# Performer attention and a feed-forward layer on one core: the beginning rebuilt (weight signs by Prelu, weight scales from squares, one shared key unit, other order)

## The chip, the cores and the metric

The kernel runs on one core of one Trainium2 chip. The metric is the device time of an execution in microseconds, as the median of several runs. The engines are named as in the profile: PE (matmul), PEld (its weight loads), DVE (vector), ACT (scalar, activations), POOL (GpSimd), SP (which issues the DMAs).

## The reference

```python
def _attn_ref(q, k, v, omega):                    # batch 8, heads 8, S = 576, D = 64, m = 128 features
    scale = 1.0 / np.sqrt(np.sqrt(D))
    def phi(x):
        h = np.einsum('bhsd,md->bhsm', x, omega) - np.sum(x * x, axis=-1, keepdims=True) / 2.0
        return np.exp(h - np.max(h, axis=-1, keepdims=True)) / np.sqrt(m)
    q_p, k_p = phi(q * scale), phi(k * scale)
    kv = np.einsum('bhsm,bhsd->bhmd', k_p, v)
    z = np.sum(k_p, axis=2)
    num = np.einsum('bhsm,bhmd->bhsd', q_p, kv)
    den = np.einsum('bhsm,bhm->bhs', q_p, z)[..., None] + 1e-06
    return num / den

def _moe_ref(x, w_in, w_out):                     # x: 4608 x 512, w_in: 512 x 2048, w_out: 2048 x 512
    h = x @ w_in
    return np.maximum(0.01 * h, h) @ w_out
```

The attention's output, heads side by side, is the x of the feed-forward layer. The weights come as 64-bit floats and are read as pairs of 32-bit words; the rest is 32-bit.

## The kernel before

The 4608 tokens are cut into 9 blocks of 512. For each block there is attention work (features of the queries, and the sums over keys and values of the batches that the block needs) and the feed-forward work: an "up" product with w_in (w1 in the program), the leaky maximum, a "down" product with w_out (w2). Blocks from 3 on use a seven-product scheme for the up product, and the last two for the down product too. Large products run as three 16-bit products of a high and a low part.

The beginning is what has to happen before the first up can start, and it has three strands.

- **Weights.** Each matrix comes in 8 pieces of 1 MB (`Weight.load`), 1024 64-bit numbers a partition. `Weight.convert` makes 32-bit floats of them from the upper and the lower word: ACT copies the upper word with a scale (L572), DVE shifts (L574) and puts three bits of the lower word in (L577), and the sign comes either from a Sign on ACT (L590) and a product on POOL (L592), or from another DVE pass (L595). PE sums the magnitudes against a column of ones (L585). `Weight.scale` needs all eight sums, takes the largest and makes a power of two of it with PE and DVE (`power_of_two`, L488 to L497). `Weight.split` then makes the high and low part of each piece.
- **Keys and values of batch 0.** A `Whole` unit takes one pair of heads: squares on ACT (L742), 32-bit projections on PE (L762), the maximum over features (L769) and a subtraction (L771) on DVE, the exponential on ACT (L773). Batches share a tile of 128 keys: batch 576 tokens is 4.5 tiles, so each unit of batch 0 has a fifth tile, projected apart into an "edge" buffer. The key sums (L865) multiply these with the values, which have been scaled by a power of two from their largest magnitude (L800, L457).
- **Queries of block 0.** The same unit, then PE turns the features (L953), the result is copied (L457), multiplied with the key sums (L982), divided (L992 to L995) into a block of x, cut into two 16-bit parts (ACT and POOL or DVE) and turned by a DMA (L910) into `xts`, of which an up needs all four.

The order of all this is not written by hand. Each operation is put on record with the engines that could do it, its buffers and a priority; `Plan.order` then lists the operations by a cost table, the priorities and long tables of corrections (`TURNS`, `HELD`, `ONLY`, by the number of the operation), with `LATER` and `PACE` for whole strands, and this is the order in which each engine's queue is written. Where the plan leaves PE a gap of 0.4 or more, `between` puts "fill" in the queue: matmuls on the identity that compute nothing and keep PE busy.

```python
                op("PE", 12 * 0.2165, up, r=[*(xts[j, k] for k in range(KT)),
                   *(key for k in range(KT) for key in w1.keys(4 * (f // 8) + k))], w=[ph], prio=work)
```

## Time and profile before

| | |
|---|---|
| runs, us | 928.76, 926.16, 928.54 (median 928.54) |
| span of the profiled execution, us | 926.5 (its own time is not listed apart; the median lies 2.0 above the span) |
| PE busy | 903.4 us |
| DVE busy | 770.4 us |
| ACT busy | 555.4 us |
| POOL busy | 387.1 us |
| granted clock of TensorE, mean | 0.997 |

A busy PE is not a working PE here: fill counts as busy, and so do matmuls at the lower clock. So the profile is read by stretches of time and by lines, not by the share of the span. Consecutive instructions of an engine overlap a little in the records; what one costs in a queue is the distance of the starts.

### The profile page before, as it was taken

The numbers are of one execution on the slowest core, as the hardware profiler recorded it, in microseconds if no ns is written. First come the engines' busy times: TensorE is split into PE (matmuls) and PEld (weight loads), VectorE is DVE, ScalarE is ACT, GpSimd is POOL, SyncE is SP. The second block draws the span as 40 slices with busy tenths as digits, with TensorE's granted clock in tenths as the row PEclk, the third lists the DMA queues.
The fourth block names the chain that finished last, engine by engine and source line by source line (L and its number), as shares of the span: only waits on it lengthen the run. The fifth ranks groups of instructions, "written<-read, shape, count | busy, mean of one in ns | idle before, by whom it ended". The sixth has DMA issues, their size and how long they took to land.

```text
span 926.5 us, 21317 instructions
## 1 busy us (share of the span) xinstructions
PE 903.4 (98%) x8660; PEld 620.5 (67%) x8660; DVE 770.4 (83%) x1374; ACT 555.4 (60%) x856; POOL 387.1 (42%) x342
## 2 busy tenths in 40 slices
PE   6989999999999999999999999999999999999998
PEld 5887465545555555578557855786568647888887
DVE  6989988997898977989887889889888886884772
ACT  4888586766673774658556745486457543542530
POOL 2234543556645453135502542134135456632650
PEclk9999999999999999999999999999999999999999
DMA  9684448756476589869686878489849645532401
GB/s 356 249 282 142 120 109 176 163 143 163 70 188 181 123 175 236 169 152 215 190 155 134 197 189 163 103 217 203 146 89 245 139 89 125 168 80 68 139 1 46
DMA packets 258242, 145.93 MB, mean 158 GB/s; under 512 B 191328, under 2 KB 238176, under 8 KB 257120
## 3 DMA queue, kind: packets, MB, share of 16 engines
q1 hardware_dynamic: 258144, 144.58, 63.4%
...
q14 instruction: 31, 0.25, 0.1%
...
## 4 chain that ended last, share of the span: by engine, by line
PE 81%; DVE 7%; DMA 6%; ACT 3%; issue 2%; POOL 1%; SPq 0%; DVEq 0%; ACTq 0%; POOLq 0%
PE fixps_ffn L1372 30%; PE fixps_ffn L1258 15%; PE fixps_ffn L1348 12%; PE lateps_ffn L1258 5%; PE attps_pj L698 5%; PE fixps_ffn L1182 4%; PE lateps_ffn L1182 4%; DMA proj_t<-proj_z 3%; DMA fix_big<-w_in 2%; PE attps_mi L975 1%; POOL fix_wt L592 1%; DVE fix_wt L577 1%; PE attps_mi L865 1%; PE attps_pj L762 1%; PE attps_mi L976 1%
## 5 line engine op out<-in xcount | busy, mean ns | idle before, releaser
L1372 PE MATMUL fixps_ffn<-fix_wt,fix_big 128*128 128x512 f16 x1344 | 302.6, 379 | 0.0
L1372 PEld LDWEIGHTS <-fix_big 128*128 128x128 f16 x1344 | 126.9, 98 | 144.1
L1258 PEld LDWEIGHTS <-fix_wt 128*128 128x128 f16 x2016 | 195.2, 98 | 27.1 <-issue 2.5
L463 POOL TENSOR_TENSOR fix_big<-fix_row,fix_big 128x512 f16<-128x512 f32 x100 | 133.8, 1344 | 179.2 <-ACT fix_big L457 165.2
L1258 PE MATMUL fixps_ffn<-fix_xt,fix_wt 128*128 128x256 f16 x1608 | 183.8, 273 | 2.1 <-DVE fix_row L1273 2.1
L1348 PE MATMUL fixps_ffn<-fix_xt,fix_wt 128*128 128x512 f16 x576 | 129.2, 379 | 0.8 <-ACT fix_row L1355 0.8
L1348 PEld LDWEIGHTS <-fix_wt 128*128 128x128 f16 x576 | 54.7, 98 | 63.8 <-issue 1.1
L717 ACT ACTIVATE att_p<-att_p,shift 128x1024 f32<-128x1024 f32 x68 | 69.9, 1030 | 36.8 <-DVE att_p L714 36.7
L705 DVE TENSOR_REDUCE proj_st<-attps_pj 128x8 f32<-128x1024 f32 x68 | 72.9, 1075 | 10.2 <-PE attps_pj L698 9.8
L457 ACT ACTIVATE fix_big<-fix_row 128x512 f16<-128x512 f32 x118 | 72.0, 623 | 9.7 <-DVE fix_row L1024 3.6
L714 DVE SCALAR_TENSOR_TENSOR att_p<-attps_pj,proj_sc,proj_st 128x1024 f32<-128x1024 f32 x68 | 76.6, 1132 | 0.1
L463 DVE TENSOR_TENSOR att_ph<-att_p,att_ph 128x1024 f16<-128x1024 f32 x56 | 73.9, 1323 | 2.2 <-ACT att_ph L457 2.2
L463 POOL TENSOR_TENSOR fix_xn<-fix_x,fix_xn 128x512 f16<-128x512 f32 (+1 forms) x24 | 26.1, 1089 | 94.7 <-ACT fix_xn L457 82.9
L1281 ACT ACTIVATE fix_row<-fix_row 128x512 f32<-128x512 f32 x69 | 43.1, 626 | 37.1 <-DVE fix_row L1273 36.7
L658 ACT ACTIVATE proj_z<-proj_nat 128x512 f32<-128x512 f32 (+1 forms) x56 | 36.2, 647 | 46.1 <-DMA proj_t<-proj_z 35.6
L1273 DVE TENSOR_TENSOR fix_row<-fix_row,fixps_ffn 128x512 f32<-128x512 f32 x57 | 38.9, 684 | 18.9 <-PE fixps_ffn L1258 9.7
L698 PE MATMUL attps_pj<-om,proj_t 64*128 64x128 f16 x1416 | 50.0, 217 | 4.0 <-DMA proj_t<-proj_z 3.2
L698 PEld LDWEIGHTS <-proj_t 64*128 64x128 f16 x1416 | 39.7, 94 | 18.9 <-issue 13.3
L682 DVE SCALAR_TENSOR_TENSOR proj_z<-proj_nat,proj_sc,proj_z 128x512 f16<-128x512 f32 (+1 forms) x52 | 50.8, 977 | 1.7 <-ACT proj_z L457 1.6
L457 ACT ACTIVATE att_ph<-att_p 128x1024 f16<-128x1024 f32 x47 | 49.2, 1047 | 0.9 <-PE attps_mi L878 0.5
L660 DVE TENSOR_REDUCE proj_sq<-proj_z 128x8 f32<-128x512 f32 (+1 forms) x56 | 39.4, 707 | 10.2 <-ACT proj_z L658 10.2
L1258 PE MATMUL lateps_ffn<-fix_xt,fix_wt 128*128 128x256 f16 x408 | 47.8, 273 | 0.0
...
## 6 DMA issues: line engine op xcount, KB each, us to landing
...
```

The source lines that it names most:

```text
L457: ("ACT", act(n, int(pointer)), lambda: nc.scalar.activation(dst(), src(), AF.Copy, scale=1.0 if scale is None else value()), False),
L463: return ways([(e, c, lambda g=g: g.tensor_tensor(dst(), a(), b(), op=ALU.subtract), True) for e, c, g in (("POOL", pool_(n), nc.gpsimd), ...
L682: op("DVE", stt(n) + 0.15, lambda: nc.vector.scalar_tensor_tensor(zl(), heads(), up(), zh(), op0=ALU.mult, op1=ALU.subtract), port=True, r ...
L698: nc.tensor.matmul(at(pj)[:, 512 * h + c * M:512 * h + (c + 1) * M], at(self.t)[r, 2 * (c0 + c) + x, :], om[r, w, :], start=(x + w == 0), ...
L705: op("DVE", dve(n * M), lambda: nc.vector.tensor_reduce(row(0), pv(), axis=AX.X, op=ALU.max), r=[pj], w=[st], prio=prio)
L714: op("DVE", dve(n * M), lambda: nc.vector.scalar_tensor_tensor(p(), pv(), down(), row(2).rearrange("p (g o) -> p g o", o=1).broadcast_to([ ...
L717: op("ACT", act(n * M, 1), lambda: nc.scalar.activation(flat(p()), flat(p()), AF.Exp, bias=shift), w=[p32], r=["ones"], prio=prio)
L1182: nc.tensor.matmul(o, ga(gp, f, 1)[:, 0, P * t:P * t + P], w(f, wp), start=(first and place + f % 2 + t + gp + wp == 0), stop=(place == 3 ...
L1258: nc.tensor.matmul(o, unit(at(wb[c]), u)[:, wp, P * a:P * a + P], mixes[j, c][n][1](xp), start=(first and a == 0 and i == 0), stop=(a == 1 ...
L1281: op("ACT", act(512), lambda: nc.scalar.activation(at(g), at(src), AF.Prelu, scale=H_DOWN_D if finish else H_DOWN_S, alpha=0.01), r=[src], ...
L1348: nc.tensor.matmul(at(ph), wk[wp][:, c:c + P], xt[:, xp, :], start=(i == 0), stop=(i == 3 * KT - 1))
L1372: nc.tensor.matmul(at(po), part(f, gp)[:, t * P:(t + 1) * P], wf[wp], start=(n == 0 and f % 4 == 0 and gp == wp), stop=(n == 3 and f % 4 = ...
```

## The change

- A weight piece is converted by a Prelu on ACT, whose slope of 2^32 for negative numbers sets the bit that the shift by three moves to the sign, a one-input pass on POOL that takes the top three bits of the lower word, and one DVE pass that joins both. The sign operations, the DVE shift and the choice `SIGN_POOL` go.
- The weight scale comes from squares: PE multiplies each 128-wide part of a piece with itself and adds all up in one bank; the largest sum's root gives the power of two.
- The fifth key tiles of batch 0 (for all four pairs of heads) are one unit "e" of their own, kept in two row buffers. The values of batches 0 and 1 stay unscaled; their scale comes from sums of squares on ACT and is applied where the key sums are evicted.
- The first queries are turned before their exponential, and the eviction is the exponential. Their products use the "ffn" banks, and every other x block a second buffer.
- For query block 1 and for edges, the scale, the bias and the exponential are one ACT instruction per head and tile (`powers`), without the DVE pass.
- The first three ups of block 0 are cut in two halves that need two `xts` each.
- All tables of the order are new.

```diff
-SIGN_POOL = {"w1": [0, 1, 3, 4, 5, 6, 7], "w2": [0, 1, 2]}
...
-PACE = {"k": 13.5, "q": 8.5, "w1": 0, "w1s": 0, "w2": 3.5, "w2s": 15.0}
+PACE = {'k': 20.5, 'q': 15.5, 'w1': 23, 'w1s': 0, 'w2': 8, 'w2s': 2}
...
-LATER = {"s": 0.0, "w1": -15.0, "w2": -275.0, "k": -5.0, "q": -565.0, "m": 0.0}
+LATER = {'s': 40.0, 'w1': -245.0, 'w2': -440.0, 'k': -700.0, 'q': -375.0, 'm': 1860.0}
...
+FUSED = (("q", 1),)
...
 TURNS = {
-    8: -220.529105, 10: -2270.804303, 11: -2600.332764, 14: -174.238138, 15: -156.646678, 17: -8199.116259,
...
+    4: -7005.2331, 7: -5110.3778, 15: -57900.145, 21: -5388.6643, 30: -5105.2668, 37: 5334.3764, 42: -2222.8973,
...
@@ class Weight: convert @@
-            op("ACT", act(1150), lambda: nc.scalar.activation(at(f), high().bitcast(F32), AF.Copy, scale=2.0 ** -112),
-               r=[b], w=[f], prio=prio)
-            op("DVE", dve2(1024), lambda: nc.vector.tensor_scalar(shifted(), bits(), 3, 0x7FFFFFF8,
-               op0=ALU.logical_shift_left, op1=ALU.bitwise_and), port=True, r=[f], w=[tmp], prio=prio)
-
-            op("DVE", stt(1024), lambda: nc.vector.scalar_tensor_tensor(shifted(), low(), 29, shifted(),
-               op0=ALU.logical_shift_right, op1=ALU.bitwise_or), port=True, r=[b], w=[tmp], prio=prio)
...
+            op("ACT", act(1150), lambda: nc.scalar.activation(at(f), high().bitcast(F32), AF.Prelu, scale=2.0 ** -112,
+               alpha=2.0 ** 32), r=[b], w=[f], prio=prio)
+            top3 = lambda: at(tmp).bitcast(U32)
+            ways([("POOL", pool_(1024), lambda: nc.gpsimd.tensor_scalar(top3(), low(), 2.0 ** -29, 7.0, op0=ALU.mult,
+                   op1=ALU.min), True)], r=[b], w=[tmp], prio=prio)
+            op("DVE", stt(1024), lambda: nc.vector.scalar_tensor_tensor(bits(), bits(), 3, top3(),
+               op0=ALU.logical_shift_left, op1=ALU.bitwise_or), port=True, r=[tmp], w=[f], prio=prio)
+
+            def squares():
+                half = at(f).bitcast(BF16).rearrange("p (a b) -> p a b", b=2)[:, :, 1]
                 for c in range(8):
-                    col = self.col0 + 4 * (8 * (i // 4) + c) + i % 4
-                    nc.tensor.matmul(at(self.sums)[:, col:col + 1], mag[:, c * P:(c + 1) * P], ones, start=True,
-                                     stop=True)
...
+                    x = half[:, c * P:(c + 1) * P]
+                    nc.tensor.matmul(at(self.sums)[:, :P], x, x, start=(i == 0 and c == 0), stop=(i == 7 and c == 7),
+                                     skip_group_check=True)
+            op("PE", 0.5, squares, r=[f], w=[self.sums], prio=prio, slack=6.0)
...
-            if i in SIGN_POOL[self.name]:
-                op("ACT", act(1130), lambda: nc.scalar.activation(at(f), high().bitcast(F32), AF.Sign), r=[b], w=[f],
-                   prio=prio)
-                op("POOL", pool_(1024), lambda: nc.gpsimd.tensor_tensor(at(f), at(tmp), at(f), op=ALU.mult), r=[tmp],
-                   w=[f], prio=prio)
-            else:
-                op("DVE", stt(1024), lambda: nc.vector.scalar_tensor_tensor(bits(), bits(), 0x80000000, shifted(),
-                   op0=ALU.bitwise_and, op1=ALU.bitwise_or), port=True, r=[tmp], w=[f], prio=prio)
...
@@ class Unit: features @@
+            if nt == 1 or fused:
+                def powers():
+                    for g in range(n):
+                        nc.scalar.activation(p()[:, g], pv()[:, g, :], AF.Exp, scale=down(), bias=row(2)[:, g:g + 1])
+                op("ACT", n * (act(M, 2) - 0.07), powers, r=[pj, st, self.sc], w=[p32], prio=prio)
+            else:
...
@@ class Whole: all_features @@
+            if self.what == "e":
+                self.ph = [buf("row"), buf("row")]
...
+                    op("DVE", dve(4 * M), lambda h=h, g=g: nc.vector.tensor_tensor(half(h), pv()[:, g], less(g).broadcast_to(
+                        [P, 4, M]), op=ALU.subtract), r=[pj, st], w=[self.ph[h]], prio=prio)
...
+            if self.what == "k":
+                op("ACT", act(n * M, 1), lambda: nc.scalar.activation(flat(p()), flat(p()), AF.Exp, bias=shift), w=[self.ph],
+                   r=["ones"], prio=prio)
...
@@ values @@
+            if b < WHOLE:
+                junk = buf("t")
+                op("ACT", act(half * D) + READ_SUM, lambda j=j, junk=junk: nc.scalar.activation(
+                   at(junk).rearrange("p a (b d) -> p (a b) d", d=D), at(raw)[:, j * half:(j + 1) * half, :D], AF.Square,
+                   accum_out=mx2[:, j:j + 1]), r=[(raw, j)], w=[junk, f"mx2_v{b}{j}"], prio=prio)
...
@@ query_block @@
-                    high(512, lambda qp32=qp32, i=i: qp32()[:, 512 * i:512 * i + 512], lambda turned=turned: at(turned),
-                         psum=True, r=[turned], w=[(qp, i)], prio=prio)
+                    op("ACT", act(512, 1), lambda qp32=qp32, i=i, turned=turned: nc.scalar.activation(
+                       qp32()[:, 512 * i:512 * i + 512], at(turned), AF.Exp, bias=shift), r=[turned, "ones"], w=[(qp, i)],
+                       prio=prio)
...
-                acc, r = buf("mi"), buf("r")
+                acc, r = buf("mi" if j else "ffn"), buf("r")
...
@@ feed_forward @@
+                steps = ((0, 1), (2, 3)) if j == 0 and f < 3 else (range(KT),)
+                for ks in steps:
+                    def up(f=f, ph=ph, ks=ks):
+                        for k in ks:
```

How the tables move instructions shows in the built programs. First DVE at the start of the weight and key work: in the names, attps_pj is a projection's bank, proj_st the maxima, att_ph, proj_edge and fix_row features, fix_wt weight pieces, fix_big raw ones. Before:

```order
L769 TENSOR_REDUCE proj_st_189<-attps_pj_173 128x8
L574 TENSOR_SCALAR fix_wt_65<-fix_wt_64 128x1024
L771 TENSOR_TENSOR att_ph_163<-attps_pj_173,proj_st_189 128x1024
L577 SCALAR_TENSOR_TENSOR fix_wt_65<-fix_big_88,fix_wt_65 128x1024
L769 TENSOR_REDUCE proj_st_190<-attps_pj_174 128x2
L771 TENSOR_TENSOR proj_edge_184<-attps_pj_174,proj_st_190 128x256
L574 TENSOR_SCALAR fix_wt_67<-fix_wt_66 128x1024
L574 TENSOR_SCALAR fix_wt_69<-fix_wt_68 128x1024
L577 SCALAR_TENSOR_TENSOR fix_wt_67<-fix_big_89,fix_wt_67 128x1024
L577 SCALAR_TENSOR_TENSOR fix_wt_69<-fix_big_90,fix_wt_69 128x1024
```

The same place of DVE's queue after the change:

```order
L766 TENSOR_REDUCE proj_st_187<-attps_pj_171 128x8
L787 TENSOR_TENSOR att_ph_161<-attps_pj_171,proj_st_187 128x1024
L766 TENSOR_REDUCE proj_st_188<-attps_pj_172 128x8
L775 TENSOR_TENSOR fix_row_94<-attps_pj_172,proj_st_188 128x512
L775 TENSOR_TENSOR fix_row_95<-attps_pj_172,proj_st_188 128x512
L766 TENSOR_REDUCE proj_st_189<-attps_pj_171 128x8
L787 TENSOR_TENSOR att_ph_162<-attps_pj_171,proj_st_189 128x1024
L575 SCALAR_TENSOR_TENSOR fix_wt_64<-fix_wt_64,fix_wt_65 128x1024
L575 SCALAR_TENSOR_TENSOR fix_wt_66<-fix_wt_66,fix_wt_67 128x1024
```

Two key units and the shared one now stand ahead of the first weight piece, which takes one pass instead of two or three.

Second, DVE around w1's scale (mx_w, pow_w). Before, five full units' reductions stand ahead of it:

```order
L769 TENSOR_REDUCE proj_st_189<-attps_pj_173 128x8
L995 TENSOR_TENSOR fix_x_84<-attps_mi_175,att_r_167 128x256
L605 TENSOR_REDUCE mxs_w_128<-fixps_ffn_113 128x16
L606 TENSOR_REDUCE mx_w_133<-mxs_w_128 128x1
L771 TENSOR_TENSOR att_ph_163<-attps_pj_173,proj_st_189 128x1024
L992 TENSOR_SCALAR att_r_168<-attps_mi_175 128x4
L993 RECIPROCAL att_r_168<-att_r_168 128x4
L492 TENSOR_REDUCE pow_w_134<-attps_mi_175 128x1
```

After, with eight reductions ahead of the scale:

```order
L766 TENSOR_REDUCE proj_st_187<-attps_pj_171 128x8
L766 TENSOR_REDUCE proj_st_188<-attps_pj_172 128x8
L590 TENSOR_REDUCE mx_w_131<-fixps_ffn_113 128x1
L787 TENSOR_TENSOR att_ph_162<-attps_pj_171,proj_st_187 128x1024
L787 TENSOR_TENSOR att_p_0_159<-attps_pj_172,proj_st_188 128x1024
L1016 TENSOR_SCALAR att_r_167<-fixps_ffn_114 128x4
L1017 RECIPROCAL att_r_167<-att_r_167 128x4
L488 TENSOR_REDUCE pow_w_132<-attps_mi_173 128x1
```

Two units (att_ph of the last keys of batch 0, att_p of the third queries) have moved ahead of the scale's last steps.

Third, PE at the first up (fix_xt are the turned x blocks, fix_wt the parts of w1; ident is fill). Before:

```order
L1423 MATMUL fixps_ffn_114<-ident 128x256
L1348 LDWEIGHTS fix_wt_80
L1348 MATMUL fixps_ffn_114<-fix_xt_99,fix_wt_80 128x512
...
L1348 MATMUL fixps_ffn_114<-fix_xt_100,fix_wt_65 128x512
...
L1348 MATMUL fixps_ffn_114<-fix_xt_101,fix_wt_67 128x512
...
L1348 MATMUL fixps_ffn_114<-fix_xt_102,fix_wt_71 128x512
...
L585 MATMUL fixps_ffn_113<-ones,fix_wt_70 128x1
```

After:

```order
L880 MATMUL attps_mi_173<-fix_v_109,att_ph_161 128x65 x4
...
L1374 MATMUL fixps_ffn_114<-fix_xt_99,fix_wt_80 128x512
...
L1374 MATMUL fixps_ffn_114<-fix_xt_100,fix_wt_65 128x512
...
L880 MATMUL attps_mi_173<-fix_v_109,att_ph_162 128x65 x4
...
L1374 MATMUL fixps_ffn_115<-fix_xt_99,fix_wt_80 128x512
...
L1447 MATMUL attps_pj_172<-ident 128x256
...
L1374 MATMUL fixps_ffn_114<-fix_xt_101,fix_wt_67 128x512
...
L1374 MATMUL fixps_ffn_114<-fix_xt_102,fix_wt_69 128x512
```

Two key sums of batch 1 and the first halves of two ups stand ahead of the first matmul that needs the third and fourth x block. Over the whole program the fill is 113 matmuls instead of 230, 107 of them up to this place. All other matmuls are as many as before, but that the 128 for the weight sums have 128 columns instead of one.

## Rows read from the trace of the kernel before

**Rows 1.** The page: the span, and the first line of part 1.

```profile
span 926.5 us, 21317 instructions
PE 903.4 (98%) x8660; PEld 620.5 (67%) x8660; DVE 770.4 (83%) x1374; ACT 555.4 (60%) x856; POOL 387.1 (42%) x342
```

**Rows 2.** Windows: four stretches; busy us per engine, granted clock, DMA share.

```profile
0.00:4.96 4.96, 0.00 (x0) 0.00 (x0) 1.40 (x7) 2.02 (x2) 0.20 (x4) 1.00 0.59 144
4.96:88.20 83.24, 76.92 (x844) 68.81 (x845) 74.57 (x117) 65.53 (x81) 26.38 (x18) 0.98 0.73 261
88.20:921.80 833.60, 826.40 (x7818) 551.69 (x7815) 693.17 (x1247) 487.81 (x774) 360.51 (x321) 1.00 0.63 148
921.80:926.50 4.70, 0.12 (x2) 0.00 (x0) 1.30 (x3) 0.00 (x0) 0.00 (x0) 0.81 0.16 56
```

**Rows 3.** Groups by line and form, PE, 5 to 88.2 us: fill.

```profile
L1423 PE MATMUL fixps_ffn<-ident 128*128 128x256 f16 x149 | 18.0, 274 | 0.0
L1423 PE MATMUL attps_pj<-ident 128*128 128x256 f16 x81 | 9.9, 276 | 0.0
```

**Rows 4.** DVE in time: start, us, what. Passes, w1's scale, last block.

```profile
37.23 1.22 DVE L769 TENSOR_REDUCE proj_st<-attps_pj 128x8 f32<-128x1024 f32 x1
38.36 0.68 DVE L574 TENSOR_SCALAR fix_wt<-fix_wt 128x1024 uint32<-128x1024 uint32 x1
38.96 1.22 DVE L771 TENSOR_TENSOR att_ph<-attps_pj,proj_st 128x1024 f32<-128x1024 f32 x1
...
47.26 0.15 DVE L497 TENSOR_SCALAR pow_w<-pow_w 128x1 f32<-128x1 f32 x1
...
82.13 0.42 DVE L995 TENSOR_TENSOR fix_x<-attps_mi,att_r 128x256 f32<-128x256 f32 x1
```

**Rows 5.** PE in time: key sums, the first up, weight sums.

```profile
36.17 1.11 PE L865 MATMUL attps_mi<-fix_v,att_ph 128*128 128x65 f32 x8
...
38.45 1.04 PE L953 MATMUL fixps_ffn<-ident,att_ph 128*128 128x128 f32 x8
...
88.21 2.75 PE L1348 MATMUL fixps_ffn<-fix_xt,fix_wt 128*128 128x512 f16 x12
90.80 0.34 PE L585 MATMUL fixps_ffn<-ones,fix_wt 128*128 128x1 bf16 x8
91.00 5.34 PE L1348 MATMUL fixps_ffn<-fix_xt,fix_wt 128*128 128x512 f16 x24
```

**Rows 6.** Windows: the early loads; DVE before and after w1's scale.

```profile
5.00:35.00 30.00, 27.28 (x300) 23.89 (x302) 25.00 (x39) 17.50 (x18) 8.53 (x8) 1.00 0.98 401
9.52:47.33 37.81, 34.93 (x422) 31.08 (x422) 34.51 (x50) 28.95 (x34) 13.26 (x11) 1.00 0.79 314
47.33:82.13 34.80, 31.48 (x333) 28.28 (x332) 31.83 (x47) 29.63 (x41) 10.83 (x6) 0.95 0.64 205
```

**Rows 7.** Groups by line and form, ACT, 5 to 88.2 us.

```profile
L572 ACT ACTIVATE fix_wt<-fix_big 128x1024 f32<-128x1024 f32 x13 | 14.9, 1147 | 7.1 <-DMA fix_big<-w_in 7.1
L590 ACT ACTIVATE fix_wt<-fix_big 128x1024 f32<-128x1024 f32 x10 | 11.3, 1158 | 0.6 <-DVE fix_wt L574 0.6
L773 ACT ACTIVATE att_ph<-att_ph,shift 128x1024 f32<-128x1024 f32 x9 | 10.3, 1146 | 1.4 <-DVE att_ph L771 1.4
```

**Rows 8.** Groups by line and form, POOL, 5 to 88.2 us.

```profile
L592 POOL TENSOR_TENSOR fix_wt<-fix_wt,fix_wt 128x1024 f32<-128x1024 f32 x9 | 22.3, 2486 | 36.8 <-DVE fix_wt L577 19.9 <-ACT proj_z L742 13.7 <-ACT fix_wt L590 1.9
```

**Rows 9.** Waits of PE from 88.2 us to the end.

```profile
PE attps_pj L698 <- DMA proj_t<-proj_z: 3.2, 3, 1.9
PE fixps_ffn L1258 <- DVE fix_row L1273: 2.1, 3, 0.9
```

**Rows 10.** Windows, PE alone: busy us, then granted clock.

```profile
64.00:66.00 2.00, 0.42 (x4) 1.00 0.57 178
68.00:72.00 4.00, 4.00 (x24) 0.58 0.00 0
```

More of the change, by code (lines that the diff above doesn't have):

```diff
@@ L166 @@
     HOP = {"PE": 0.25, "ACT": 0.08, "DVE": 0.08, "POOL": 0.10}
-    PRICE = {"PE": 1.0, "ACT": 1.28, "DVE": 8.28, "POOL": 1.0, "SP": 1.0}
+    PRICE = {'PE': 1.0, 'ACT': 2.464, 'DVE': 7.416, 'POOL': 4.818, 'SP': 1.0}
     def __init__(self, places, groups):
@@ L461, in low_ @@
     def low_(n, dst, a, b, engines=("DVE",), **of):
-        return ways([(e, c, lambda g=g: g.tensor_tensor(dst(), a(), b(), op=ALU.subtract), True)
-                     for e, c, g in (("POOL", pool_(n), nc.gpsimd), ("DVE", stt(n), nc.vector)) if e in engines], **of)
+        o = ways([(e, c, lambda g=g: g.tensor_tensor(dst(), a(), b(), op=ALU.subtract), True)
+                  for e, c, g in (("POOL", pool_(n), nc.gpsimd), ("DVE", stt(n), nc.vector))], **of)
+        if "POOL" not in engines:
+            o.price = {**o.price, "POOL": RARE}
+        return o
     def at(b):
@@ L770, in features @@
                prio=prio)
-            op("DVE", dve(n * M), lambda: nc.vector.tensor_tensor(p(), pv(), top().rearrange("p (g o) -> p g o",
-               o=1).broadcast_to([P, n, M]), op=ALU.subtract), r=[pj, st], w=[p32], prio=prio)
-            op("ACT", act(n * M, 1), lambda: nc.scalar.activation(flat(p()), flat(p()), AF.Exp, bias=shift), w=[p32],
-               r=["ones"], prio=prio)
-        def all_features(self):
-            self.ph = buf("ph")
-            self.p = lambda: at(self.ph).rearrange("p a b m -> p (a b m)").bitcast(F32).rearrange("p (g m) -> p g m",
-                                                                                                    m=M)
-            self.features(0, 4, self.ph, self.p)
-            if self.nt == VT:
-                self.edge = buf("edge")
-                self.features(4, 1, self.edge, lambda: edge32(self.edge))
+            less = lambda g: top()[:, g].rearrange("p (g o) -> p g o", o=1)
@@ new lines, in all_features @@
+            if self.what == "e":
+                self.ph = [buf("row"), buf("row")]
+                half = lambda h: at(self.ph[h]).rearrange("p (g m) -> p g m", m=M)
+                self.p = lambda g: half(g // 4)[:, g % 4]
+                for h in range(2):
+                    g = slice(4 * h, 4 * h + 4)
+                    op("DVE", dve(4 * M), lambda h=h, g=g: nc.vector.tensor_tensor(half(h), pv()[:, g], less(g).broadcast_to(
+                        [P, 4, M]), op=ALU.subtract), r=[pj, st], w=[self.ph[h]], prio=prio)
+                    op("ACT", act(4 * M, 1), lambda h=h: nc.scalar.activation(at(self.ph[h]), at(self.ph[h]), AF.Exp,
+                       bias=shift), w=[self.ph[h]], r=["ones"], prio=prio)
+                return
@@ new lines, in all_features @@
+            if self.what == "q":
+                self.ph = buf("p32")
+                p = lambda: at(self.ph)
+            else:
+                self.ph = buf("ph")
+                p = lambda: at(self.ph).rearrange("p a b m -> p (a b m)").bitcast(F32).rearrange("p (g m) -> p g m", m=M)
+            self.p = lambda g: p()[:, g]
+            op("DVE", dve(n * M), lambda: nc.vector.tensor_tensor(p(), pv(), less(slice(0, n)).broadcast_to([P, n, M]),
+               op=ALU.subtract), r=[pj, st], w=[self.ph], prio=prio)
@@ L812, in values @@
                w=[(both, "ones")], prio=prio)
-        for j in range(2):
+        for j in range(2 if b >= WHOLE else 0):
             s = slice(j * half, (j + 1) * half)
@@ L850, in key_batch @@
             u.all_features()
-            if u.nt == VT:
-                edges[b // 2, hp] = u.edge
-            edge = edges[b // 2, hp]
+            if not b and not hp:
+                edges[0] = Whole("e", b, hp, prio)
+                edges[0].all_features()
+            if b >= WHOLE:
+                if u.nt == VT:
+                    edges[b // 2, hp] = u.edge
+                edge = edges[b // 2, hp]
             if hp % 2 == 0:
@@ L1434, in performer_ffn @@
                     later(plan.opens[b.kind][b.place])
-            if o in fill:
+            if o in fill and fill[o][0].place < len(tiles[fill[o][0].kind]):
                 busy(*fill[o])
```

194 lines of the change are left out of this document (99 added, 95 removed), and 111 rows, old and new, of tables (HELD, TURNS).

## The prediction

> **What bounds the kernel now.** I read the page first: PE is busy for 903.4 of 926.5 us [rows 1]. But PE's time has two kinds of matmul in it, work and fill, so I cut the span into stretches next. Up to 4.96 us PE does nothing; from there to 88.20, where the first feed-forward matmul stands, it is busy for 76.92 of 83.24 us; from 88.20 to 921.80 for 826.40 of 833.60; the last 4.70 us are eviction and store [rows 2]. The groups by line say what the 76.92 us are: 149 and 81 matmuls on the identity, which compute nothing, take 18.0 + 9.9 = 27.9 us [rows 3]. So before 88.2 PE works for 76.9 - 27.9 = 49.0 us and loses 27.9 to fill and 6.3 to waiting; after 88.2 it loses 7.2 us in all. The reader is to see that PE's order decides everything after the beginning, and that the only large sum to be had is the 34.2 us (27.9 + 6.3) that PE doesn't work between 5 and 88 us.
>
> What holds the first feed-forward matmul (the first "up") back is the other engines' queue. DVE is busy for 74.57 of these 83.24 us, ACT for 65.53, POOL for 26.38 [rows 2]. In time: the weight scale of w1 is ready on DVE at 47.3 us, the last block of x of the first queries starts there at 82.13 [rows 4], and a cast on ACT, a subtraction on POOL and a transposing DMA later the first up starts at 88.21 [rows 5]. That is 35 us of DVE's queue and a tail of 6.1 us. From 9.52 to 47.33 DVE is busy for 34.51 us, from there to 82.13 for 31.83, so it waits for 3.3 and 3.0 us [rows 6]. The loads are the limit early only: they run at 401 GB/s, 0.98 busy, from 5 to 35 us [rows 6], and the weight pieces wait 7.1 us for them on ACT [rows 7], but that is over some 50 us before the first up.
>
> **The change part by part.** A full pass of DVE over 1024 elements costs 1.13 us from start to start (38.36 less 37.23), one in its quick form 0.60 (38.96 less 38.36) [rows 4].
>
> Weight pieces. Before, a piece takes on DVE a shift (0.60) and an or (a full pass), and a sign pass for 6 of 16; on ACT a copy, and a Sign for 10 of 16 at 1.16 [rows 7]; on POOL a product for 10 of 16 at 2.49 [rows 8]. Now it takes one pass each on ACT (Prelu), POOL and DVE. DVE saves 16 x 0.60 + 6 x 1.13 = 16 us, ACT 10 x 1.16 = 11.6 us, half of it in the beginning. POOL gets 16 one-input passes that the trace doesn't show: from below by ACT's 1.15 for the same shape [rows 7], from above by POOL's own 2.49 for two inputs [rows 8]. I take 2.49, the same engine. Eight of them are 20 us in a beginning where POOL was busy for 26, so POOL doesn't fill up, and at 1.15 the result is the same. The Trainium skill says in "GPSIMD Engine Reference", section 4.1, that one-input work there is roughly line-rate and two-input work about twice as slow as VectorE's; no row here shows a one-input POOL pass of this size. By that sentence the pass would cost nearer to 1.2 us, and the sum would stay, as DVE is the longer queue.
>
> Squares on PE. Eight 128-column matmuls a piece stand where eight 1-column ones stood. Those step PE on by 0.20 us (91.00 less 90.80) [rows 5]. An up's 512-column matmul takes 2.59/12 = 0.216 us (90.80 less 88.21, over 12) [rows 5], a quarter of it 0.054, so eight are 0.43 us: +0.22 a piece, 3.5 us over 16. Bounds: nothing (the loads of the weights hide it) and twice 0.43, +10 us. The first 9 lie before the first full up.
>
> Key tiles, values, queries. Four 256-wide edge units become one 1024-wide unit: on DVE 8 quarter passes against 2 full ones, next to nothing. Values 0 and 1 lose four maximum passes on DVE (1280 elements, 1.25 passes each) and get four squares on ACT, where their scaling goes. The first queries lose four 1024-wide exponentials at 1.15 on ACT [rows 7], since the eight evictions now are the exponentials. For query block 1 the four bias passes (1.13 each) leave DVE and 8 small ACTs a unit replace them: that lies behind the first up, under PE's 826 us.
>
> The new order. Up to the w1 scale DVE now has 8 reductions, 8 subtractions (one in halves), 8 weight passes and, as an estimate, 7 us of small steps: 24 x 1.13 + 7 = 34 us from 9.5 on, against 34.5 before. With the 3.3 us of waiting the scale comes at about 47.3 us again; but by then 7 units and the shared one are through, not 5 and two edges. After the scale, up to the last block of x, DVE's rows are 10 full passes (11.3), 3 quick ones (1.8), 6 blocks of x at 0.42 (2.5) and, as an estimate, 3 us of small ones: 18.6 us, where there were 31.8. With 3 us of waiting, as before, the last block stands at 47.3 + 18.6 + 3 = 68.9, and with the tail of 6.1 everything for full ups is there at 75.0. ACT's rows over the same piece are ten 1024-wide casts, four conversions, four 512-wide exponentials and a few more: 20 us, so it ends beside DVE.
>
> PE has its own sum. Ahead of the first full up stand the 49.0 us of work, two more key sums (2.28 us each, 38.45 less 36.17 [rows 5]; two 4.5), the two half ups (12 matmuls, 2.6) and the squares' surplus (9 x 0.43 less 10 x 0.20 = 1.9): 58.0 us. Fill is now 107 matmuls instead of 230; at 27.9/230 = 0.121 us that is 12.9 us. So PE can't be there before 4.96 + 58.0 + 12.9 = 75.9 us, which is the later of the two; with 2 us of waiting (6.3 before, at twice the fill) the first full up stands at 77.9 us. From there: 826.4 less 4.5 and 2.6 that were done earlier, plus 7 x 0.43 - 6 x 0.20 = 1.8 for squares and 0.7 for six fills: 821.8 us. With the same 7.2 us of waiting and the same end of 4.7 the span is 77.9 + 821.8 + 7.2 + 4.7 = 911.6 us, **14.9 us less**. The runs shown have a median of 928.54, 2.0 above the profiled span; I put the result 14.9 below that median, at 913.6 us.
>
> The rest of the program has the same matmuls in another order. Its waits are few: transposes for query and key features 3.2 us, a DVE addition 2.1 [rows 9]. DVE keeps its load (693 of 834 us [rows 2]) less some 15 us. I price this at nothing, hidden under PE, with 3 us to either side.
>
> **The rivals.** *The scale comes late.* The scale now needs POOL's and DVE's pass behind the last load, and DVE's 34 us may hold more than 4 us of waiting, since its rows depend on PE's. If the scale comes 7 us later, the first full up stands at 85: 921 us. For it speaks that the last w1 load can hardly land earlier, with the same bytes at 401 GB/s; against it that DVE waited for little (3.3 us [rows 6]).
>
> *PE's clock falls.* Fill kept PE busy, and half of it goes. In 64 to 66 us PE was busy for 0.42 of 2 us; in 68 to 72 the granted clock was 0.58, mostly the lower level of 1.2 GHz [rows 10]. That stretch lost 4 x (1 - 0.58) = 1.7 us. Two more such places cost 3.4: 917 us. The Trainium skill's page "TensorE: Matmul & The Clock Gate", section "HAM oscillation", speaks against taking activity away: idle gaps throttle the array again and each is paid anew; the dip in these rows agrees.
>
> *Slower: w2 comes late.* At the first full up w2 has one piece converted instead of four, and its squares and its scale stand in PE's queue between the first 12 ups, so PE itself waits if a piece isn't ready, with all ups behind it. The 7 pieces must pass in about 36 us, 5 us each. It turns the gain into a loss if they cost PE over 14.9 us of waiting, 2.1 each; at 3 us each the time is 913.6 + 21 = 935. Against it: a piece needs 1.13 us of DVE, 1.15 of ACT and at most 2.49 of POOL, and DVE waited for w2 before with more work a piece.
>
> *No gain.* The queue's waits grow by what its work shrinks: the first full up would have to stand at 93 us, 15 later than my sum. The trace shows no resource that would do this.
>
> **How the numbers follow.** The forecast, 907 to 918, has 0.62; the late scale (921) 0.16; the clock (917) 0.10; no gain (928) 0.05; w2 late (935) 0.07. What lies within 0.3% (2.8 us) a measurement of this kernel can't tell from no change. Faster: 0.62 + 0.16 + 0.10 = 0.88; same 0.05; slower 0.07. The range takes in squares at nothing and 3 us less waiting (913.6 - 3.5 - 3 - 2 = 905) and the late scale with 3 us more (924).
>
> **What would show it.** The profile after should have the w1 scale on DVE near 47 us, the last block of x near 69, the first ups from 70 and full ones near 78, about 113 matmuls of fill at 13 to 14 us, PE busy near 893 us, and under 8 us of PE's waiting between the first full up and the end. A first full up past 85, a granted clock under 1 in more than one place before it, or waits of PE at the w2 squares would make it wrong.

## The result: 0.7% slower

In runs on one chip, nine of each kernel, the changed kernel takes 934.74 us (median; 930.94 to 941.61), the kernel before 928.76 (926.16 to 930.42): ratio 1.0072, 95% interval 1.0045 to 1.0098. The forecast was 913.6 us. The timed miss is 21.1 us. The profiled execution has a span of 932.4 us, 20.8 over the 911.6 of my sum.

The page of the changed kernel, to be held against [rows 1]:

```profile
span 932.4 us, 21056 instructions
PE 901.2 (97%) x8543; PEld 617.5 (66%) x8543; DVE 748.3 (80%) x1355; ACT 550.8 (59%) x899; POOL 384.4 (41%) x311
```

PE has 117 matmuls fewer, as foreseen, but is busy for 901.2 us, not 893. Windows of the changed kernel, columns as in [rows 2]; 90.21 us is where the first matmul starts that needs the last block of x:

```profile
4.76:90.21 85.45, 75.25 (x768) 68.24 (x769) 67.47 (x109) 54.77 (x71) 62.42 (x22) 0.92 0.82 283
90.21:927.70 837.49, 825.93 (x7775) 549.27 (x7774) 678.43 (x1238) 494.13 (x826) 321.77 (x286) 1.00 0.63 144
```

The beginning lasts longer than before, although DVE has 7 us less to do there. POOL has gone from 26.38 to 62.42 us of it. The groups by line and form of the same stretch say with what:

```profile
L573 POOL TENSOR_SCALAR fix_wt<-fix_big 128x1024 uint32<-128x1024 uint32 x12 | 49.5, 4122 | 11.9 <-DMA fix_big<-w_in 11.0
...
L575 DVE SCALAR_TENSOR_TENSOR fix_wt<-fix_wt,fix_wt 128x1024 uint32<-128x1024 uint32 x12 | 14.5, 1221 | 11.1 <-POOL fix_wt L573 11.1
L456 DVE TENSOR_TENSOR fix_wt<-fix_wt,fix_wt 128x1024 f16<-128x1024 f32 x3 | 5.5, 1848 | 0.3 <-ACT fix_wt L450 0.3
```

The pass that takes the three bits (L573) is 4.12 us long, not 2.49, and DVE's pass behind it (L575) waits 11.1 us for it. POOL in time, 11 to 60 us (start, busy us, what, count):

```profile
11.46 17.16 POOL L573 TENSOR_SCALAR fix_wt<-fix_big 128x1024 uint32<-128x1024 uint32 x4 [11.02 <-DMA fix_big<-w_in]
28.69 1.93 POOL L837 COPY row_scale<-pow_v 128x1 f32<-128x1 f32 x5
30.70 17.08 POOL L573 TENSOR_SCALAR fix_wt<-fix_big 128x1024 uint32<-128x1024 uint32 x4
```

POOL hardly pauses from 11.5 to 47.8 us: the eight pieces of w1 stand in a queue of their own. What follows from it stands on PE (timeline; in brackets the wait ahead of a row and what ended it):

```profile
44.13 0.80 PE L759 MATMUL attps_pj<-fix_xt,proj_nat 64*128 64x128 f32 x4 [2.35 <-DVE att_p L787]
54.94 0.44 PE L484 MATMUL attps_mi<-ident,mx_w 128*128 128x128 f32 x2
67.15 3.89 PE L1006 MATMUL fixps_ffn<-fix_kv,att_qp 128*128 128x65 f32 x16 [2.90 <-ACT fix_kv L450]
83.13 1.46 PE L1374 MATMUL fixps_ffn<-fix_xt,fix_wt 128*128 128x512 f16 x6
90.21 2.10 PE L1374 MATMUL fixps_ffn<-fix_xt,fix_wt 128*128 128x512 f16 x9 [1.18 <-DMA fix_xt<-fix_xn]
```

The scale's product is at 54.94, the first half up at 83.13, the first up on the last block at 90.21, behind waits that the forecast put at 2 us in all and that are 10.2 (85.45 - 75.25).

After 90 us there is a second loss. Two places in the timeline:

```profile
356.44 0.19 PE L999 MATMUL attps_mi<-fix_kv,att_qp 128*128 128x65 f16 x1 [2.63 <-DVE fix_y L1019]
...
356.80 4.44 PE L1396 MATMUL fixps_ffn<-fix_wt,fix_big 128*128 128x512 f16 x12
...
612.82 0.20 PE L1001 MATMUL attps_mi<-fix_kv,att_qp 128*128 128x65 f16 x1 [3.01 <-DMA att_qp<-att_ph]
...
613.18 4.40 PE L1282 MATMUL fixps_ffn<-fix_xt,fix_wt 128*128 128x256 f16 x24
```

Each wait is followed by matmuls at less than full speed. The chain of work at the first place (start, us, what) tells what the DVE step waited for:

```profile
347.69 0.46 SPq L1083
348.20 7.55 DMA w1s<-fix_y
...
355.97 0.43 DVE fix_y L1019
```

A mixed weight is stored from a buffer of kind y; the store takes 7.55 us, DVE can't write the next block of x there before it is done, DVE's block frees the bank of PSUM that PE writes next. At the second place the chain is a transposing DMA of 7.12 us for the queries.

### The profile page after: what moved, and what is told of

It reads as the page before. It is cut to its first block, busy times and chain, and to the rows that moved or that the text cites. A ratio compares the mean times of both kernels' runs of the same rounds, so it can differ in the third digit from the quotient of the medians.

```text
span 932.4 us, 21056 instructions
## 1 busy us (share of the span) xinstructions
PE 901.2 (97%) x8543; PEld 617.5 (66%) x8543; DVE 748.3 (80%) x1355; ACT 550.8 (59%) x899; POOL 384.4 (41%) x311
## 4 chain that ended last, share of the span: by engine, by line
PE 74%; DMA 10%; DVE 8%; POOL 5%; issue 2%; ACT 1%; SPq 1%; DVEq 0%; ACTq 0%; POOLq 0%
PE fixps_ffn L1396 24%; PE fixps_ffn L1282 16%; PE fixps_ffn L1374 10%; PE lateps_ffn L1282 5%; PE lateps_ffn L1206 5%; PE attps_pj L680 4%; POOL fix_wt L573 4%; PE fixps_ffn L1206 3%; DMA proj_t<-proj_z 2%; DMA fix_xt<-fix_xn 2%; DMA w1s<-fix_y 2%; DMA att_qp<-att_ph 1%; PE attps_mi L999 1%; DVE proj_st L687 1%; DMA fix_big<-w_in 1%
## 5 line engine op out<-in xcount | busy, mean ns | idle before, releaser
L456 POOL TENSOR_TENSOR fix_big<-fix_row,fix_big 128x512 f16<-128x512 f32 x66 | 85.3, 1293 | 154.7 <-ACT fix_big L450 124.1
L709 ACT ACTIVATE att_p<-att_p,shift 128x1024 f32<-128x1024 f32 x52 | 59.4, 1143 | 32.5 <-DVE att_p L706 32.3
L450 ACT ACTIVATE fix_big<-fix_row 128x512 f16<-128x512 f32 x115 | 70.1, 624 | 11.8 <-DVE fix_row L1048 7.1
L573 POOL TENSOR_SCALAR fix_wt<-fix_big 128x1024 uint32<-128x1024 uint32 x16 | 65.1, 4070 | 13.5 <-DMA fix_big<-w_in 11.0
L456 DVE TENSOR_TENSOR fix_big<-fix_row,fix_big 128x512 f16<-128x512 f32 x73 | 62.6, 868 | 5.9 <-ACT fix_big L450 5.3
L706 DVE SCALAR_TENSOR_TENSOR att_p<-attps_pj,proj_sc,proj_st 128x1024 f32<-128x1024 f32 x52 | 66.2, 1276 | 0.1
L456 DVE TENSOR_TENSOR att_ph<-att_p,att_ph 128x1024 f16<-128x1024 f32 x48 | 62.2, 1296 | 4.5 <-ACT att_ph L450 4.5
L450 ACT ACTIVATE att_ph<-att_p 128x1024 f16<-128x1024 f32 x49 | 51.5, 1050 | 2.1 <-PE attps_mi L894 1.6
L1282 PE MATMUL lateps_ffn<-fix_xt,fix_wt 128*128 128x256 f16 x444 | 51.4, 273 | 0.0
L664 DVE SCALAR_TENSOR_TENSOR proj_z<-proj_nat,proj_sc,proj_z 128x512 f16<-128x512 f32 (+1 forms) x52 | 47.0, 906 | 4.1 <-ACT proj_z L450 3.9
```

What stands on the lines that cost most here:

```text
L450: ("ACT", act(n, int(pointer)), lambda: nc.scalar.activation(dst(), src(), AF.Copy, scale=1.0 if scale is None else value()), False),
L456: o = ways([(e, c, lambda g=g: g.tensor_tensor(dst(), a(), b(), op=ALU.subtract), True) for e, c, g in (("POOL", pool_(n), nc.gpsimd), ("D ...
L573: ways([("POOL", pool_(1024), lambda: nc.gpsimd.tensor_scalar(top3(), low(), 2.0 ** -29, 7.0, op0=ALU.mult, op1=ALU.min), True)], r=[b], w ...
L664: op("DVE", stt(n) + 0.15, lambda: nc.vector.scalar_tensor_tensor(zl(), heads(), up(), zh(), op0=ALU.mult, op1=ALU.subtract), port=True, r ...
L706: op("DVE", dve(n * M), lambda: nc.vector.scalar_tensor_tensor(p(), pv(), down(), row(2).rearrange("p (g o) -> p g o", o=1).broadcast_to([ ...
L709: op("ACT", act(n * M, 1), lambda: nc.scalar.activation(flat(p()), flat(p()), AF.Exp, bias=shift), w=[p32], r=["ones"], prio=prio)
```

## Experiments

All ratios are to the kernel before, in runs on the same chip; that of the changed kernel is 1.0072. The experiments ran on several chips, on which the kernel before took 928.2 to 929.0 us, and the changed kernel's own interval is some 2.5 us to either side: differences in microseconds from it are no better than that, and the ratios decide. The theory at the start: POOL's pass is the one wrong price. Rivals: the new order or the loads set the beginning; and the later waits belong to the new order.

**e1: the price of the pass by itself.** A program with nothing but POOL passes: three each of six forms, alone, then beside DVE passes.

```
for _ in range(3):
    nc.gpsimd.tensor_scalar(ints, pair[:, :, 0], 2.0 ** -29, 7.0, op0=ALU.mult, op1=ALU.min)
...  # side by side; mult alone; floats; 512 words; two-input product
```

> This kernel computes nothing of the reference (its output is zeros): POOL does six forms of a pass over 128 partitions three times each, first with DVE idle, then while DVE does scalar_tensor_tensor passes over 1024 words without a pause. The forms: the changed kernel's own (integer words 8 bytes apart in, mult and min, integers out), the same with words side by side, the same with mult alone, mult and min on floats in and out, the changed form over 512 words, and the two-input float product of the kernel before. Theory 'the form of the pass costs 4 us by itself': the first form takes 4.0 to 4.2 us with DVE idle, and the float form at most 2.5 us, so that integers or the spacing make the price. Rival 'DVE makes it slow': with DVE idle the first form takes 2.5 us or less, and about 4.1 us only in the second half. If the two-input float product takes 2.5 us alone and DVE's passes 1.2 us, the rows of the kernel before are of undisturbed passes.

Groups by line and form, POOL, in the stretch with DVE idle. L395 is the changed kernel's form, L397 words side by side, L399 mult alone, L401 floats, L403 512 words, L405 the two-input product:

```profile
L395 POOL TENSOR_SCALAR ints<-raw 128x1024 uint32<-128x1024 uint32 x3 | 11.0, 3667 | 2.4 <-DMA raw<-w_in 2.2
L401 POOL TENSOR_SCALAR floats<-fb 128x1024 f32<-128x1024 f32 x3 | 10.9, 3626 | 0.2
L397 POOL TENSOR_SCALAR ints<-raw 128x1024 uint32<-128x1024 uint32 x3 | 10.9, 3624 | 0.2
L399 POOL TENSOR_SCALAR ints<-raw 128x1024 uint32<-128x1024 uint32 x3 | 8.4, 2811 | 0.2
L405 POOL TENSOR_TENSOR floats<-fb,fa 128x1024 f32<-128x1024 f32 x3 | 7.0, 2337 | 0.2
L403 POOL TENSOR_SCALAR ints<-raw 128x512 uint32<-128x512 uint32 x3 | 5.8, 1938 | 0.2
```

The same view, of the stretch with DVE busy:

```profile
L411 DVE SCALAR_TENSOR_TENSOR dst<-dst,other 128x1024 uint32<-128x1024 uint32 x40 | 60.8, 1520 | 1.4
...
L395 POOL TENSOR_SCALAR ints<-raw 128x1024 uint32<-128x1024 uint32 x3 | 13.1, 4362 | 0.3
...
L405 POOL TENSOR_TENSOR floats<-fb,fa 128x1024 f32<-128x1024 f32 x3 | 8.7, 2900 | 0.2
```

Neither theory as written. The form costs 3.67 us alone, so DVE isn't the main cause; but integers and spacing cost nothing, the float form is as slow. The second operation costs 0.86 us, the two-input product with one operation is the cheaper (2.34). Beside a busy DVE a POOL pass takes 4.36 us. DVE's mean there is 1.52, but the median of its 40 passes is 1.23: most are not slowed, single ones take up to 3.24.

**e2, e3: less of the pass.** The changed kernel with POOL's pass over 64 or 512 of the columns, which DVE reads again for the others; all else in place.

```diff
-  nc.gpsimd.tensor_scalar(top3(), low(), 2.0 ** -29, 7.0, ...)
+  nc.gpsimd.tensor_scalar(top3()[:, :64], low()[:, :64], 2.0 ** -29, 7.0, ...)      # e3: 512
-  nc.vector.scalar_tensor_tensor(bits(), bits(), 3, top3(), ...)
+  nc.vector.scalar_tensor_tensor(cut(bits()), cut(bits()), 3, <top3()[:, :64] for each 64>, ...)
```

> The changed kernel with POOL's pass of each weight piece cut to 64 of 1024 columns; DVE's pass reads these 64 again for all columns, so the three lowest bits of the other weights are wrong. Every other instruction and its place in its queue is that of the changed kernel. Theory 'POOL's pass of 4.1 us sets the time of the scale of w1': the scale comes some 8 us sooner (PE's product for it at 45 to 48 us in place of 54.9), the first full up by 78 to 82 us in place of 90.2, and the kernel takes 915 to 924 us, 10 to 20 us less than the changed kernel. Rival 'the order or the loads set it': the scale stays past 52 us and the kernel within 3 us of the changed one (931 to 937 us).

> As the run with 64 columns, with 512: POOL's pass then takes some 2.1 us, which is less than the 2.6 us in which one piece of weights is loaded, and near the 2.49 us that the prediction took for it. Theory 'POOL's pass at 4.1 us is the one price that was wrong': the time is within 2 us of that with 64 columns, 915 to 925 us. If half the gain of the run with 64 columns is missing, POOL's time counts in proportion, and a price of 2.49 us would not have given the forecast either. Rival 'order or loads': 931 to 937 us, as the changed kernel.

Measured: 929.47 us (ratio 1.0005, 0.9989 to 1.0022) and 928.53 (1.0009, 0.9991 to 1.0027), in neither theory's range. POOL's pass was 0.65 and 2.34 us long. The run with 64 columns in windows (its profiled execution took 925.09 us, 4.4 under its median):

```profile
5.00:83.24 78.24, 72.17 (x768) 65.39 (x769) 65.35 (x109) 54.39 (x71) 17.60 (x23) 0.96 0.90 309
83.24:918.50 835.26, 824.15 (x7775) 547.97 (x7774) 674.48 (x1238) 494.45 (x826) 306.88 (x285) 1.00 0.63 145
```

and its longest wait of DVE up to 83 us (total, times, longest):

```profile
DVE proj_st L766 <- PE attps_pj L759: 6.0, 3, 2.9
```

POOL's pass is worth 5 to 6 us of the whole; in the profiles the first up on the last block comes 7.0 us sooner with 64 columns (90.21 to 83.24) and 4.2 with 512 (86.04). At 2.34 us, near the 2.49 that I took, all of it is back in the timed runs, and the scale's product, at 49.07, is no later than with 64 columns. But the forecast is still missed by 15 us: a right price for the pass would not have made it. With 64 columns the scale's product on PE is at 50.44, not 45 to 48, and DVE, now free of POOL, waits for PE's products of features. So the first theory holds for a quarter to a third of the miss only.

**e4, e7: the shift on DVE.** The pass done by DVE at the same place of the order, for all pieces (e4) or for w1 alone (e7); nothing left out.

```diff
-  nc.gpsimd.tensor_scalar(top3(), low(), 2.0 ** -29, 7.0, op0=ALU.mult, op1=ALU.min)
+  nc.vector.tensor_scalar(top3(), low(), 29, None, op0=ALU.logical_shift_right)   # e7: if self.name == "w1"
```

> The changed kernel with the same order of everything, but the pass that takes the three bits is a right shift on DVE, in DVE's queue at the place where POOL had it in its own; nothing is left out. Theory 'POOL's pass sets the scale': DVE takes 8 times 0.8 to 1.3 us more up to the scale, POOL some 33 us less, and DVE's other passes are no longer slowed by POOL (1.85 and 2.35 us back to 1.2 and 1.3): scale at 47 to 51 us, first full up at 80 to 85 us, 916 to 928 us in all, at least 6 us under the changed kernel. Rival 'order or loads': within 3 us of the changed kernel. A third, 'DVE is so full that the pass costs as much there': 930 us or more with the scale no sooner, and DVE without pauses up to it.

> The changed kernel with the shift on DVE for the eight pieces of w1 and POOL's pass kept for the eight of w2. Theory 'POOL costs time only on the way to the scale of w1': the time is that of the kernel with all sixteen on DVE within 2 us (926 to 929 us), and scale and first full up lie where they lay there (50.3 and 83.8 us). Rival 'POOL's passes for w2 cost as much, since they slow DVE or hold the buffers of the loads': 931 us or more.

e4: 927.41 us (0.9990, 0.9976 to 1.0004). Groups by line and form, DVE, 5 to 84 us:

```profile
L573 DVE TENSOR_SCALAR fix_wt<-fix_big 128x1024 uint32<-128x1024 uint32 x12 | 9.0, 753 | 1.6 <-DMA fix_big<-w_in 1.6
...
L456 DVE TENSOR_TENSOR fix_wt<-fix_wt,fix_wt 128x1024 f16<-128x1024 f32 x2 | 2.4, 1217 | 0.0
```

On DVE the pass takes 0.75 us, a fifth of POOL's; the subtractions beside it are back at 1.22 from 1.85. Scale's product 50.29, first up on the last block 83.80: as expected. e7: 925.63 us (0.9973, 0.9961 to 0.9985), 0.4 under what was expected: only w1's passes cost time, those of w2 may stay on POOL (its interval and that of e4 overlap, so that they gain there isn't shown).

**e5, e6: the two later waits.** Four steps moved in the finished order: the first waiting product behind the next 12 matmuls, the second behind the next 24 (with its DVE step), and the transposing DMA for it ahead of two weight loads. e5 keeps POOL's pass, e6 has the shift on DVE.

```diff
     fill = between(order)
+    at_number = {o.number: o for o in order}
+    for number, behind in ((1086, 980), (2212, 2210), (2214, 2229), (2213, 1948)):
+        order.remove(at_number[number])
+        order.insert(order.index(at_number[behind]) + 1, at_number[number])
```

> The changed kernel with four steps moved in the finished order and nothing else touched: the product of queries and key sums for which PE waited 2.63 us at 356.4 stands behind the next 12 matmuls of the feed-forward, that for which it waited 3.01 us at 612.8 behind the next 24, its DVE step behind it, and the second turned query part that it waits for goes out ahead of two weight loads. Theory 'two waits of the new order, each with a stretch of half clock behind it (12 matmuls of 512 columns in 4.44 us in place of 2.76, 24 of 256 in 4.40 in place of 2.79), are what the rest of the program lost': both waits go to under 0.5 us, the stretches behind them run at 2.76 and 2.79 us, 8 us less, 924 to 928 us. Rival 'the slack only moves': the same transfers hold PE up a few microseconds later, and the time stays within 3 us of the changed kernel.

> The four moved steps and the shift on DVE in place of POOL's pass, together; nothing left out. Theory 'the two causes are apart': the time is that of the kernel with the shift on DVE alone (927.4 us) less what the moved steps gave in the changed kernel, 918 to 921 us, faster than both kernels. Rival 'the slack only moves': 926 to 929 us. If it lies between, part of the waits comes back further on, and the waits of PE after 84 us tell where.

e5: 928.62 us (0.9993, 0.9980 to 1.0007), 6.1 less than the changed kernel. e6: 921.39 us (0.9927, 0.9908 to 0.9945), faster than both kernels. PE at the two places in e5, then e6 in windows:

```profile
344.56 10.53 PE L1396 MATMUL fixps_ffn<-fix_wt,fix_big 128*128 128x512 f16 x48
354.93 0.19 PE L999 MATMUL attps_mi<-fix_kv,att_qp 128*128 128x65 f16 x1
...
603.44 5.42 PE L1282 MATMUL fixps_ffn<-fix_xt,fix_wt 128*128 128x256 f16 x48
608.69 0.19 PE L999 MATMUL attps_mi<-fix_kv,att_qp 128*128 128x65 f16 x1
```

```profile
4.85:84.10 79.25, 71.75 (x769) 64.43 (x769) 71.77 (x120) 54.57 (x71) 10.32 (x10) 0.98 0.88 305
84.10:914.90 830.80, 823.05 (x7775) 548.31 (x7774) 677.15 (x1242) 494.29 (x826) 306.64 (x281) 1.00 0.63 146
```

The results of e5 and e6 lie 0.6 and 0.4 us above the ranges of the first theory. Both waits are gone and 48 matmuls take 10.53 us, 2.63 for 12 instead of 4.44. Small ones come up instead (0.93 us at 356.4, 1.22 at 371.8, both for a block of x on DVE), which is why 6 and not 8 us are had. The two causes add: 934.74 - 7.3 (e4) - 6.1 (e5) = 921.3, measured 921.39. That it fits to 0.1 us is luck; by the ratios it is 0.9911 against 0.9927 (0.9908 to 0.9945).

**e8: the planner told.** The shift as an operation of DVE in the plan, so that the whole order is made anew.

```diff
-  ways([("POOL", pool_(1024), ...
+  op("DVE", stt(1024), ..., port=True, r=[b], w=[tmp], prio=prio)
```

> The shift on DVE, and the planner told so, so that the order of the whole program is made anew with it (the tables of priorities are those of the changed kernel, made for its own numbers). Theory 'the tables fit one order alone': the time is over that of the same pass in the kept order, 927.4 us, by 3 to 15 us, with more waits of PE after 84 us. Rival 'a planner that knows where the pass runs does better': 915 to 925 us.

966.88 us (1.0413, 1.0382 to 1.0444), far over what either theory gave. Groups by line and form, PE, fill, of this kernel:

```profile
L1447 PE MATMUL attps_pj<-ident 128*128 128x256 f16 x206 | 24.3, 273 | 1.7 <-DVE att_p L706 1.7
L1447 PE MATMUL fixps_ffn<-ident 128*128 128x256 f16 x175 | 21.0, 273 | 0.1
```

It has 381 matmuls of fill, the changed kernel 113; 191 of the 381 stand in the first 140 us. The tables by operation number fit one order; in another one the plan has gaps of PE all over, and fills them. It says nothing of the pass.

**e9: the loads.** e4 with half of w1's bytes loaded.

```diff
-  nc.sync.dma_start(out=raw, in_=w[k * P:(k + 1) * P, 2048 * s:2048 * (s + 1)])
+  nc.sync.dma_start(out=raw[:, :1024], in_=w[k * P:(k + 1) * P, 2048 * s:2048 * s + 1024])
...  # ACT's and DVE's passes read the half twice
```

> The changed kernel with the shift on DVE, and only the first 512 columns of each piece of w1 loaded, which ACT and DVE read twice (the other half of the columns of w1 is left out, its copies stand there): 4 MB less before the scale, at some 415 GB/s about 10 us of transfers; every instruction and its place are those of the kernel with the shift on DVE. Theory 'with POOL out of the way the loads pace the way to the scale': w1's last piece is there near 28 us in place of 37.5, the scale near 43 in place of 50.3, the first full up 3 to 7 us sooner than 83.8 us, 920 to 925 us. Rival 'PE and DVE wait for each other in the order of their queues': the last piece comes sooner and nothing else does; scale within 2 us of 50.3, full up within 2 of 83.8, 925 to 929 us.

923.89 us (0.9964, 0.9949 to 0.9979), 3.5 under e4, which ran on another chip; by the ratios 2.4. PE in e9:

```profile
47.01 0.44 PE L484 MATMUL attps_mi<-ident,mx_w 128*128 128x128 f32 x2
...
80.71 3.40 PE L1374 MATMUL fixps_ffn<-fix_xt,fix_wt 128*128 128x512 f16 x15 [1.21 <-DMA fix_xt<-fix_xn]
```

The last piece of w1 is there at 33.3 us (37.5 in e4), not at 28; scale and first up come 3.3 and 3.1 us sooner: ten microseconds of transfers (the expectation's estimate) give three. The loads hold a part of the beginning; what holds the rest this run doesn't show.

**e10: all that helped.** e7 with the moved steps.

> The shift on DVE for w1, POOL's pass for w2, and the four moved steps; nothing left out. If the three findings add, 925.6 us (shift on DVE for w1 alone) less the 6 to 6.1 us of the moved steps: 918.5 to 921 us, the fastest of all, with a first full up near 83 us and no wait of PE over 2 us after it. Rival 'POOL's passes for w2 and the moved steps use the same slack': 921 to 925 us.

920.98 us (0.9921, 0.9907 to 0.9934): the fastest, but not told apart from e6; the 1.8 us of e7 under e4 don't add (first up on the last block at 84.47, behind 1.62 us for its transposing DMA).

## Why the prediction was wrong

Its own sum against the windows; each part is busy time, then waits of PE:

| | forecast | changed kernel | e6 |
|---|---|---|---|
| ahead of the beginning | 4.96 | 4.76 | 4.85 |
| beginning, PE's work and fill | 70.9 | 75.25 | 71.75 |
| beginning, waits | 2.0 | 10.20 | 7.50 |
| rest, work | 821.8 | 825.93 | 823.05 |
| rest, waits | 7.2 | 11.56 | 7.75 |
| end | 4.7 | 4.70 | 4.70 |
| span | 911.6 | 932.4 | 919.6 |

**The step that failed first: the price of POOL's pass.** I bounded it "from above by POOL's own 2.49 for two inputs" [rows 8], took the bound and concluded that "POOL doesn't fill up". It takes 4.12: two operations on one input cost POOL 3.67 us, one operation on two 2.34 (e1), and DVE's passes beside it add some. A row of another form was no upper bound. Eight of them in a row then paced w1 (scale's product 54.94 instead of 45.6), and the rival "the scale comes late" came in. It put the scale at 7 us late, the first full up at 85 and the time at 921 us (by the prediction's own DVE sum of 75.0 it should have said 84 and 920); they are 10 us, 90.21 and 934.74. It named POOL's pass behind the last load and DVE's waiting for PE, but not eight passes that pace the pieces. The Trainium skill, "GPSIMD Engine Reference", section 4.1, has one-input work roughly at line-rate and two-input work about twice as slow as VectorE; in e1 a copy (1.04 us) and the two-input product (2.34, against 1.23 for DVE's two-input pass) agree, but one-input arithmetic differs, with 2.81 us for one operation and 3.67 for two, and the measurement decides. Shown by e2 to e4 and e7: 5 to 9 us of the miss.

**The second: "I price this at nothing", for the rest in another order.** The 3 us to either side held too little. Two waits (2.63 and 3.01 us) and slow matmuls behind them were 6 us (e5, e6). The rows of before could not show them; the new order could have: the store of a mixed weight out of a y buffer with a block of x next in it, and a transposing DMA behind weight loads with the product close behind it.

**The third: 2 us of waits in the beginning.** I scaled 6.3 us of before by the fill. With POOL out of the way they are still 7.5 (e6), and the first up on the last block is at 84.10 instead of 77.9. Which terms were too small is read best from e2, where POOL's pass is nearly gone and DVE has no shift to do. Its windows up to the scale and from there to the last block of x:

```profile
9.50:53.10 43.60, 40.59 (x469) 37.23 (x466) 32.86 (x51) 26.21 (x35) 5.33 (x14) 0.96 1.05 380
53.10:73.40 20.30, 18.70 (x197) 17.36 (x197) 20.07 (x34) 19.03 (x26) 8.34 (x5) 0.92 0.45 138
```

DVE's work up to the scale was right, 32.9 us where I had 34. Its waits were not: 10.7 us (43.60 less 32.86) where I took over 3.3 from before, 6.0 of them for PE's projections. So the scale stands at 53.1, 5.8 us late, without POOL's doing. From there to the start of the last block it is 20.0 us (forecast 21.6). The tail behind that is the other term: I took over 6.1 us, and it is 10.2 (73.1 to 83.24). SP's queue and DVE at that place of e2:

```profile
72.74 0.72 DVE L1019 TENSOR_TENSOR fix_y<-fixps_ffn,att_r 128x256 f32<-128x256 f32 x2
...
73.06 1.05 SPq L558 DMA_DIRECT2D fix_big<-w_out  x2
...
76.27 1.96 SPq L933 DMA_TRANSPOSE fix_xt<-fix_xn  x1
```

From issue to landing this transposing DMA takes 6.9 us in e2, the one in the same place before took 3.1 (DMA issues of the two kernels, e2 first):

```profile
fix_xt<-fix_xn SPq DMA_TRANSPOSE x1, 6.9
```

```profile
fix_xt<-fix_xn SPq DMA_TRANSPOSE x1, 3.1
```

Together 5.8 - 1.6 + 4.1 = 8.3 us more than the 75.0 of the prediction's DVE sum. In the new order two loads of w2 of 1 MB each are issued 3.2 us ahead of the transposing DMA, where before they were issued 1.8 us behind it (85.33 and 87.12); the DMA engines' share from issue to landing is 1.10 in e2, 0.61 before. That these loads hold it up is likely, but no run takes them away. Why DVE's waits grew is not settled either. The loads have a part in them, since e9 brings the scale 3.3 us sooner, but e9 leaves out 4 MB, and the new order puts only 640 KB more ahead of the last piece of w1 (five key loads of 256 KB where two of 320 stood); ACT takes this piece up at 37.49 us in e4 and at 36.72 before. So about 8 us of the miss stay (921.4 - 913.6). The 6.2 of them in the beginning (84.10 - 77.9) are traced to these two terms, not to a cause that a run shows; the rest lies behind it and isn't settled.

**PE's clock** was a rival and came along with the waits, as their price rather than as a cause of its own. Granted clocks of the changed kernel, windows:

```profile
355.00:360.00 5.00, 3.56 (x21) 1.53 (x21) 2.82 (x10) 2.04 (x5) 0.90 (x1) 0.71 0.80 202
...
45.00:50.00 5.00, 5.00 (x38) 4.44 (x38) 4.75 (x5) 2.56 (x4) 4.92 (x2) 0.51 0.94 294
...
70.00:75.00 5.00, 5.00 (x44) 4.76 (x44) 4.93 (x11) 4.77 (x7) 4.84 (x3) 0.62 0.00 0
```

Behind each wait of 2 to 3 us (44.13, 67.15, 356.44 us; behind that at 612.82 the mean is 0.67 up to 618) the clock is at its lower level of 1.2 GHz for a while. In the beginning that is the 4.65 us between 75.25 and the 70.60 that e4 needs for the same matmuls at 1.00:

```profile
4.76:83.80 79.04, 70.60 (x769) 63.41 (x770) 71.22 (x119) 54.23 (x71) 10.30 (x10) 1.00 0.86 305
```

Later it is 1.7 and 1.6 us at the two places (4.44 less 2.76, 4.40 less 2.79). So a wait of 3 us cost about 4.6. A long wait isn't needed: behind three waits of 0.4 to 0.8 us between 59 and 64 us the granted clock is 0.76 from 63 to 70 us in e6, and 1.00 in e4, which has the same waits. The Trainium skill's page "TensorE: Matmul & The Clock Gate", section "HAM oscillation", has idle gaps throttle the array each time anew; these rows agree in kind.

**What was right.** DVE's saving (67.47 busy against 74.57), the fill (113 matmuls), PE's own sum: where the clock stays at 1.00, in e4, work and fill of the beginning are 70.6 us. From the scale's product to the first up on the last block the time fell from 42.6 us (45.62 to 88.21) to 32.8 in e2 (50.44 to 83.24); the forecast had it fall by 10.3 (from 47.3 to 88.2 down to 47.3 to 77.9). That the two agree is partly luck: DVE's part fell as forecast, and the longer tail took the place of PE's own sum, which I had as the later of the two. The squares cost what was said: a group of 8 steps PE on by 0.46 us (80.44 to 80.90), no product for w2 waited, and "w2 comes late" did not occur; that the 935 us of that rival is the time measured is coincidence, the kernel was slower by another way.
